# Three first-layer blocks before the first second-layer block, channels 128 to 191 convolved in two token halves, operands in named homes

## The chip, the core and the metric

The kernel runs on one core of a Trainium2 chip. The metric is the device time of one execution in microseconds. The kernel before takes 1253.04 us, the median of three runs (1252.96 to 1254.81).

## What is computed

A causal depthwise convolution (7 taps, softmax of a weight per head, 8 heads of 24 channels) over 2 x 4096 tokens of 192 channels, then two layers on the 8192 tokens, all in float32:

```
w = softmax(weight, axis=-1)                       # (8, 7)
x[t, c] = sum_k w[head(c), k] * x_pad[t + k, c]    # causal, zeros ahead of the first token
g = x @ w_gate ; val = x @ w_val                   # 192 -> 1536 each
y = (silu(g) * val) @ w_out                        # 1536 -> 192
h = y @ w_in                                       # 192 -> 2048
out = where(h > 0, h, exp(min(h, 0)) - 1) @ w_out2 # 2048 -> 192
```

## The kernel before

The 8192 tokens are cut into 16 blocks of 512 (TB). Each block goes through layer 1 (called A0 to A15 here: 12 steps, one for each 128 columns of d_ff) and layer 2 (B0 to B15: 8 steps of two such groups). Channels lie on partitions, tokens along the free axis.

Every float32 operand of a matmul is split in two fp32r parts, hi and lo (a cast on ACT, then a subtraction on DVE), and three products hi*hi, hi*lo, lo*hi are summed in PSUM. An operand x or y of a block is a pair of tiles with three slots of 512 columns: slot 0 holds channels 0 to 127, slot 1 the same channels with the two 64-partition halves swapped (two transfers from SBUF to SBUF, `turn`, L417), slot 2 channels 128 to 191 on both halves. A step of a layer issues nine pairs of matmuls into PSUM (`Into.nine`, L316), one matmul of a pair on the lower and one on the upper 64 rows of the array, then the activation and the split of h (`swiglu` and `elus`, `split`: L535, L539, L569 to L581, L509, L513), and two steps later the five pairs of the output product of each group (`OutOf.ten`, L358). A layer-1 block therefore has 12 x 18 + 12 x 10 matmuls, a layer-2 block 8 x 18 + 16 x 10.

The weights arrive as 34 pieces of int64 words (float64 in memory), which `piece` turns into fp32r hi and lo parts on the chip: transfers by the SP queue (L235), one scaling on ACT (L239), a shift, a sign and a low-bits step on DVE (L243, L247, L253), then hi on ACT (L258) and lo on DVE (L261). Pieces 0 to 17 belong to layer 1, 18 to 33 to layer 2. All of them have to be through once; this is work of the first 165 us only.

`load_x` brings a block of x into the tile xs (L438, L440; 128 channels in one transfer, channels 128 to 191 twice, to both halves), `conv` runs seven taps over it for g = 0 (channels 0 to 127) and g = 1 (channels 128 to 191, the same numbers on both halves of the partitions): the last tap on ACT (L466), six on DVE (L469), each 128x512.

The order of all instructions is written by a planner, `Plan`. Each piece of work is a task with an engine, a cost (`pitch`, the time that it holds its engine, and `ready`, the time until its result can be used) and its dependences; `Plan.run` hands out tasks engine by engine in the order of a simulated time, the one with the longest remaining chain first. PE's tasks keep the order in which they were written, which is that of the list `stages` (L685): A0, A1, B0, A2, B1, A3, B2 and so on up to A15, B14, B15. On the chip every engine then follows its own list in order and waits by semaphores. Buffers are rings: the tiles of all x and y share a ring of three (`x_p`), reused in the order in which they were made; PSUM has 4 banks for the first products, xs 2 tiles, the words 4.

Of the kernel before, what the change touches and what calls it, by code (L numbers as in the profile page):

```python
# [126 lines left out]
def tile_conv_swiglu_elu(ctx: ExitStack, tc: tile.TileContext, x, weight, words, out, FF1, FF2):  # L127
# [8 lines left out]
    G = D // H  # L136
    HALO = K - 1
    NU = {1: FF1 // P, 2: FF2 // P}
    assert D == P + HALF
# [80 lines left out]
    def piece(moves, halves, serves):  # L220

        k = len(pieces)
        pieces.append(k)
        st_b, f_b = plan.buffer("ws", 4), plan.buffer("wf", 4)
        box = {}

        def bring(i):
            if i == 0:  # L230
                box["st"] = ws_p.tile([P, C, 2], I32, tag="ws", name=f"words{k}")
            (r, g), (r_in, g_in) = moves[i]
            w = words[k].rearrange("p (g c w) -> p g c w", g=3, w=2)
# [29 lines left out]
        came = [  # L263
            move(lambda i=i: bring(i), new=[st_b] if i == 0 else (), uses=[] if i == 0 else [st_b], ready=3.6)
            for i in range(len(moves))
        ]
        for i in came[1:]:
            i.behind.append(came[0])
        t = act(scale, came, new=[f_b], uses=[st_b], pitch=0.45, ready=0.6)
        t = dve(shift, [t], uses=[f_b], pitch=0.29, ready=0.4)  # L270
        t = dve(sign, [t], uses=[f_b, st_b], pitch=0.49, ready=0.6)
        t = dve(low, [t], uses=[f_b, st_b], pitch=0.49, ready=0.6)
        his, los = [], []
        for pick, hi, lo in halves:
# [96 lines left out]
    class Operand:  # L371

        def __init__(self, name):
            self.name = name
            self.bufs = [plan.buffer(f"x{q}", 3) for q in ("hi", "lo")]
            self.tiles = [None, None]
            self.slots = {}

        def make(self, q):
            self.tiles[q] = x_p.tile([P, 3, TB], F32R, tag=f"x{'hi lo'.split()[q]}", name=f"{self.name}{q}")

        def write(self, s, value, needs, uses, n):

# [23 lines left out]
            if s == 0:  # L409
                for q, done in ((0, h), (1, l)):  # L410
# [2 lines left out]
                        for r, r_in in ((lower, upper), (upper, lower))  # L413
                    ]

    def turn(t, r, r_in, n):
        nc.sync.dma_start(out=raw(t[r, 1, :n]), in_=raw(t[r_in, 0, :n]))  # L417

    def load_x(b):
        i, t0, n = blocks[b]  # L420
        a = HALO if t0 == 0 else 0
        c = slice(t0 - HALO + a, t0 + n)
        buf = plan.buffer("xs", 2)
        box = {}

        def make():
            box["t"] = xs_p.tile([P, 2, HALO + TB], F32, tag="xs", name=f"xs{b}")

        def pad():
            make()  # L430
            nc.gpsimd.memset(box["t"][:, :, 0:a], 0.0)

        def bring(k):
            if k == 0 and not a:
                make()
# [6 lines left out]
        padded = [pool(pad, new=[buf], pitch=0.1, ready=0.2)] if a else []  # L442
        came = []
        for k in range(3):
            new = [buf] if k == 0 and not a else []
            came.append(move(lambda k=k: bring(k), new=new, uses=[] if new else [buf], ready=3.4))
            if k:
                came[k].behind.append(came[0])
            came[k].behind += padded
        xs[b] = box, buf, [padded + came[:1], padded + came[1:]]  # L450

    X = {}

    def conv(b, g):

        n = blocks[b][2]
        src, src_b, came = xs[b]
        acc_b = plan.buffer("cv", 2)
        box = {}

        def tap(k, eng=None):
            s = src["t"][:, g, k : k + n]
            w = taps[:, g, k : k + 1]
            if k == HALO:
                box["acc"] = cv_p.tile([P, TB], F32, tag="cv", name=f"cv{b}_{g}")
                nc.scalar.mul(box["acc"][:, :n], s, w)  # L466
                return
            acc = box["acc"][:, :n]
            nc.vector.scalar_tensor_tensor(out=acc, in0=s, scalar=w, in1=acc, op0=ALU.mult, op1=ALU.add)  # L469

        t = act(lambda: tap(HALO), came[g], new=[acc_b], uses=[src_b], pitch=0.62, ready=0.78)
        for k in range(HALO):
            t = dve(lambda k=k: tap(k), [t], uses=[src_b, acc_b], pitch=0.67, ready=0.8)
        if g == 0:
            X[b] = Operand(f"x{b}")
        X[b].write(2 * g, lambda: box["acc"][:, :n], [t], [acc_b], n)


    Y = {}
# [144 lines left out]
    def middle(b, *ends):  # L624
        n = blocks[b][2]
        (s1, b1, o1), (s2, b2, o2) = gathered((1, b), (f"y1_{b}", f"y2_{b}"), ((o_p, "o1"), (y_p, "y")), ends, n)
        Y[b] = Operand(f"y{b}")
# [54 lines left out]
        conv(0, g)  # L682
    load_table(AF.Silu)

    stages = [(1, 0)]  # L685
    for b in range(NB):
        if b + 1 < NB:
            stages.append((1, b + 1))
        stages.append((2, b))
    steps = [[]]  # L690
    for i, (layer, b) in enumerate(stages):
        if layer == 1 and b + 1 < NB:
            load_x(b + 1)
            for g in range(2):
                conv(b + 1, g)
# [8 lines left out]
        for u in us:  # L704
            products_out(u)

    plan.run({"pe": 5.0, "act": 5.0, "dve": 5.0, "pool": 3.0, "sp": 0.6}, PATIENCE)


# [43 lines left out]
```

## Time and profile before

| | |
|---|---|
| median of three runs | 1253.04 us |
| the profiled execution | 1253.94 us, of which span 1252.1 us |
| PE busy | 1216.1 us, 97% of the span |
| DVE busy | 1011.8 us, 81% |
| ACT busy | 822.7 us, 66% |

PE is the TensorE matmul engine, PEld its weight loads, DVE the vector engine, ACT the scalar engine, SP the queue that issues the transfers. Busy shares are means over a start-up and a steady part that have different limits, so the profile is read by stage below. "us" in a row is a length, the first number of a timeline row its start. In the views by stretch, x counts the instructions that touch the stretch, those at its edges too; PEclk is the granted TensorE clock as a share of 2.4 GHz.

### The profile page before, as it was taken

Reading aid. Unit: us, or ns where it says so; the run is one execution under the profiler, and the core shown is the slowest. Engines: PE = TensorE matmul, PEld = TensorE weight load, DVE = VectorE, ACT = ScalarE, POOL = GpSimd, SP = SyncE. Lnnn points to the kernel's source line nnn. Section 1 sums busy time; section 2 is a strip of 40 time slices with the busy share of each in tenths; the row PEclk is TensorE's granted clock in tenths of the full one; section 3 lists DMA queues with packets and bytes.
Section 4 is the critical chain, followed back from the end, with each engine's and each line's share of the span. In section 5 each row is a group of like instructions: output and inputs, shape, how many; then the busy total and the mean of one; then the engine's idle time right before and its main releaser. Section 6 shows DMA issues by size and latency. Waiting matters only on the chain.

```text
span 1252.1 us, 25084 instructions
## 1 busy us (share of the span) xinstructions
PE 1216.1 (97%) x10244; PEld 1127.8 (90%) x10244; DVE 1011.8 (81%) x1661; ACT 822.7 (66%) x1505; POOL 1.6 (0%) x11
## 2 busy tenths in 40 slices
PE   4989899999999999999999999999999999999998
PEld 3568689889999999999899999999999999999996
DVE  7999997979779596986959789695977959485697
ACT  4567757658476584857758486674857658485675
POOL 0000000000000000000000000000000000000000
PEclk9989999999999999999999999999999999999999
DMA  6433111111101010010101001010100101000000
GB/s 170 138 102 119 47 39 44 30 44 35 31 18 43 5 35 31 18 47 18 31 19 35 31 18 48 3 41 22 28 20 19 31 1 35 14 18 14 15 13 18
DMA packets 29795, 46.53 MB, mean 37 GB/s; under 512 B 4848, under 2 KB 12528, under 8 KB 29680
## 3 DMA queue, kind: packets, MB, share of 16 engines
q1 hardware_dynamic: 29664, 44.93, 13.7%
q8 instruction: 80, 1.31, 0.4%
q14 instruction: 35, 0.29, 0.1%
q10 hardware_dynamic: 16, 0.00, 0.0%
HBM read 21.84 MB, written 6.29 MB: 22 GB/s over the span
## 4 chain that ended last, share of the span: by engine, by line
PE 87%; DVE 9%; DMA 1%; issue 1%; ACT 1%; SPq 0%; DVEq 0%; ACTq 0%
PE c L358 38%; PE ph L316 19%; PE pv L316 16%; PE pg L316 14%; DVE cv L469 2%; DVE t L581 1%; DVE h L513 1%; DVE t L577 1%; DMA words<-in_words_dram 1%; DVE w L253 1%; DVE w L247 1%; DVE t L539 0%; DVE w L243 0%; DVE out L261 0%; SPq L235 0%
## 5 line engine op out<-in xcount | busy, mean ns | idle before, releaser
L358 PE MATMUL c<-h,out 64*128 64x512 f32 x4480 | 620.5, 393 | 8.8 <-DVE out L261 4.2
L358 PEld LDWEIGHTS c<-h,out 64*128 64x128 f32 x4480 | 515.8, 185 | 47.7 <-DVE h L513 9.4
L316 PE MATMUL pg<-x,in1hi 64*128 64x512 f32 x1152 | 394.7, 396 | 15.9 <-ACT in1hi L258 15.2
L316 PE MATMUL pv<-x,in1hi 64*128 64x512 f32 x1152 | 395.3, 397 | 0.1
L509 ACT CAST h<-t 128x512 fp32r<-128x512 f32 x448 | 280.0, 627 | 161.6 <-DVE t L539 138.6
L513 DVE TENSOR_TENSOR h<-t,h 128x512 fp32r<-128x512 f32 x448 | 307.5, 686 | 92.3 <-ACT h L509 90.8
L316 PE MATMUL ph<-y,in2hi 64*128 64x512 f32 x1536 | 307.4, 393 | 1.4 <-DVE t L581 1.1
L316 PEld LDWEIGHTS pg<-x,in1hi 64*128 64x128 f32 x1152 | 214.9, 187 | 28.0 <-ACT in1hi L258 16.7
L316 PEld LDWEIGHTS ph<-y,in2hi 64*128 64x128 f32 x1536 | 218.7, 184 | 12.9 <-DVE t L581 3.8
L316 PE MATMUL pg<-x,in1lo 64*128 64x512 f32 x576 | 228.8, 397 | 0.3
L316 PE MATMUL pv<-x,in1lo 64*128 64x512 f32 x576 | 228.4, 397 | 0.0
L316 PEld LDWEIGHTS pv<-x,in1hi 64*128 64x128 f32 x1152 | 215.4, 187 | 9.9 <-DVE t L539 0.8
L539 DVE TENSOR_TENSOR t<-t,pv 128x512 f32<-128x512 f32 x192 | 131.2, 683 | 112.8 <-ACT t L535 112.6
L535 ACT ACTIVATE t<-pg 128x512 f32<-128x512 f32 x192 | 114.7, 597 | 160.1 <-PE pg L316 137.4
L316 PE MATMUL ph<-y,in2lo 64*128 64x512 f32 x768 | 205.6, 392 | 0.0
L569 ACT ACTIVATE th<-ph 128x512 f32<-128x512 f32 x256 | 155.6, 608 | 50.0 <-PE ph L316 41.7
L577 DVE SCALAR_TENSOR_TENSOR t<-t,th 128x512 f32<-128x512 f32 x256 | 171.7, 685 | 15.2 <-ACT t L573 15.2
L581 DVE SCALAR_TENSOR_TENSOR t<-ph,t 128x512 f32<-128x512 f32 x256 | 170.0, 685 | 2.0
L573 ACT ACTIVATE t<-ph 128x512 f32<-128x512 f32 x256 | 155.3, 607 | 0.0
L469 DVE SCALAR_TENSOR_TENSOR cv<-xs,taps,cv 128x512 f32<-128x512 f32 x192 | 139.0, 743 | 3.9 <-ACT cv L466 2.8
L316 PEld LDWEIGHTS ph<-y,in2lo 64*128 64x128 f32 x768 | 120.5, 185 | 3.9 <-DVE in2lo L261 0.6
L316 PEld LDWEIGHTS pg<-x,in1lo 64*128 64x128 f32 x576 | 107.6, 187 | 7.9 <-DVE in1lo L261 3.3
(47 smaller groups left out, 501.1 us busy)
## 6 DMA issues: line engine op xcount, KB each, us to landing
x<-x SPq DMA_DIRECT2D x64, 128.0 KB, 2.3
y<-y SPq DMA_DIRECT2D x64, 128.0 KB, 2.3
words<-in_words_dram SPq DMA_DIRECT2D x14, 384.0 KB, 3.2
words<-in_words_dram SPq DMA_DIRECT2D x40, 128.0 KB, 2.8
out_dram<-o SPq DMA_DIRECT2D x16, 256.0 KB, 2.0
xs<-in_x_dram SPq DMA_DIRECT2D x14, 259.0 KB, 2.9
xs<-in_x_dram SPq DMA_DIRECT2D x28, 129.5 KB, 3.2
words<-in_words_dram SPq DMA_DIRECT2D x40, 64.0 KB, 2.5
```

Source lines behind the costliest of these rows:

```text
L247: nc.vector.scalar_tensor_tensor(out=i, in0=box["st"][:, :, 1], scalar=-(2**31), in1=i, op0=ALU.bitwise_and, op1=ALU.bitwise_or)
L316: nc.tensor.matmul(p[:, :n], w[r, k, s], m[r, s, :n], start=i == 0, stop=i == len(seq) - 1)
L358: nc.tensor.matmul(p[:, :n], lhs[r], m[r, :n], start=first, stop=last)
L469: nc.vector.scalar_tensor_tensor(out=acc, in0=s, scalar=w, in1=acc, op0=ALU.mult, op1=ALU.add)
L509: nc.scalar.copy(parts[u][0][:, :n], live[u][0]["t"][:, :n])
L513: nc.vector.tensor_tensor(out=parts[u][1][:, :n], in0=live[u][0]["t"][:, :n], in1=raw(parts[u][0][:, :n]), op=ALU.subtract)
L535: nc.scalar.activation(out=box["t"][:, :n], in_=box["p"][0][:, :n], func=AF.Silu)
L539: nc.vector.tensor_tensor(out=t, in0=t, in1=box["p"][1][:, :n], op=ALU.mult)
L569: nc.scalar.activation(out=own["th"][:, :n], in_=box["p"][a][:, :n], func=AF.Tanh, scale=0.5)
L573: nc.scalar.activation(out=own["t"][:, :n], in_=box["p"][a][:, :n], func=AF.Exp)
L577: nc.vector.scalar_tensor_tensor(out=t, in0=t, scalar=1.0, in1=th, op0=ALU.add, op1=ALU.mult)
L581: nc.vector.scalar_tensor_tensor(out=t, in0=box["p"][a][:, :n], scalar=0.0, in1=t, op0=ALU.max, op1=ALU.min)
```

## The change

Three things change, and with them the planner's order of nearly all instructions.

The list `stages` gets a lead of three: A0, A1, A2, B0, B1, A3, B2, A4, B3 and on as before. Against the list before, A2 and B0 change places; from A3 on the two are the same.

Channels 128 to 191 are convolved in halves of the tokens: xs holds the first 256 tokens of a block on partitions 0 to 63 and the second 256 on partitions 64 to 127, so that the six taps of g = 1 are 128x256 and the tap on ACT too. `spread` then writes hi and lo of the two halves in place (two casts on ACT and two subtractions on DVE, each 64x256), and four transfers from SBUF to SBUF copy each half to the other 64 partitions. Before, the same slot took one cast and one subtraction of 128x512 and no transfer.

Operand tiles are no longer a ring: `settle` gives every x and y one of three homes by the stage in which the earlier occupant is last used. The planner also charges a transfer with 0.62 instead of 0.4 us of SP's time.

```
+LEAD = 3
-    x_p = ctx.enter_context(tc.tile_pool(name="xp", bufs=3))
+    x_p = ctx.enter_context(tc.tile_pool(name="xp", bufs=1))
-    def move(emit, needs=(), new=(), uses=(), pitch=0.4, ready=2.8):
+    def move(emit, needs=(), new=(), uses=(), pitch=0.62, ready=2.9):
...
+            self.bufs = [plan.buffer(f"x{q}{home}", 1) for q in ("hi", "lo")]
...
+        def spread(self, value, done, buf, n):
+            half = n // 2
+            places = (lower, slice(0, half)), (upper, slice(half, n))
+            first = self.slots[0, 0][0], self.slots[1, 0][0]
+            his, los = [], []
+            for r, c in places:
+                def hi(r=r, c=c):
+                    nc.scalar.copy(self.tiles[0][r, 2, c], value()[r, :half])
+                def lo(r=r, c=c):
+                    nc.vector.tensor_tensor(
+                        out=self.tiles[1][r, 2, c], in0=value()[r, :half], in1=raw(self.tiles[0][r, 2, c]), op=ALU.subtract
+                    )
+                h = act(hi, [done], uses=[self.bufs[0], buf], pitch=0.33, ready=0.45)
+                l = dve(lo, [done, h], uses=[*self.bufs, buf], pitch=0.34, ready=0.47)
...
+            for q, own in enumerate((his, los)):
+                other = []
+                for (r, c), (r_in, _), t in zip(places, places[::-1], own):
+                    def send(q=q, r=r, c=c, r_in=r_in):
+                        nc.sync.dma_start(out=raw(self.tiles[q][r_in, 2, c]), in_=raw(self.tiles[q][r, 2, c]))
+                    other.append(move(send, [t], uses=[self.bufs[q]]))
+                self.slots[q, 2] = [*own, *other]
...
         def bring(k):
-            if k == 0 and not a:
-                make()
-            t = box["t"]
             if k == 0:
-                nc.sync.dma_start(out=t[:, 0, a : HALO + n], in_=x[i, 0:P, c])
-            else:
-                nc.sync.dma_start(out=t[(lower, upper)[k - 1], 1, a : HALO + n], in_=x[i, P:D, c])
+                box["t"] = xs_p.tile([P, 2 * HALO + TB + TB // 2], F32, tag="xs", name=f"xs{b}")
+            skip = a if k < 2 else 0
+            first, m = (0, n) if k == 0 else ((k - 1) * half, half)
+            rows = slice(0, P) if k == 0 else slice(P, D)
+            src = x[i, rows, t0 + first - HALO + skip : t0 + first + m]
+            nc.sync.dma_start(out=at(k, skip, HALO + m), in_=src)
...
+        m, c0 = ((n, 0), (n // 2, HALO + TB))[g]
...
+    stages = [(1, b) for b in range(min(LEAD, NB))] + [(2, b) for b in range(LEAD - 1)]
+    for b in range(LEAD - 1, NB):
+        if b + 1 < NB:
+            stages.append((1, b + 1))
+        stages.append((2, b))
+    home, last = {}, {}
+    for i, (layer, b) in enumerate(stages):
+        last["xy"[layer - 1], b] = i
+    holds = [None] * 3
+    def settle(what, i):
+        free = [h for h in range(3) if holds[h] is None or last[holds[h]] < i]
+        home[what] = h = max(free, key=lambda h: last[holds[h]] if holds[h] else -1)
+        holds[h] = what
...
-    stages = [(1, 0)]
-    for b in range(NB):
-        if b + 1 < NB:
-            stages.append((1, b + 1))
-        stages.append((2, b))
```

What the planner makes of it is seen at three places. Names are tiles: wordsN and wN are weight piece N as words and on the way to fp32r, xsN the input of block N, cvN_g its convolution, x0N the hi and x1N the lo tile of block N, h1_L_b_j the lo part of group j of block b in layer L, t the activation, in1, in2, out1, out2 the finished weights.

The first transfers of the SP queue, before: words of the first pieces (seven transfers in all), then the input.

```order
L235 DMA words1_135<-in_words_dram 64x2x256
L235 DMA words1_135<-in_words_dram 64x256
L235 DMA words1_135<-in_words_dram 64x2x256
L438 DMA xs0_139<-in_x_dram 128x512
L440 DMA xs0_139<-in_x_dram 64x512 x2
```

And now, from the first transfer on:

```order
L474 DMA xs0_130<-in_x_dram 128x512
L474 DMA xs0_130<-in_x_dram 64x256
L474 DMA xs0_130<-in_x_dram 64x262
L236 DMA words0_134<-in_words_dram 64x2x256
L236 DMA words0_134<-in_words_dram 64x256
```

The input now goes first, the first words behind it.

DVE at the end of the first convolution, before (the shift and the sign of piece 0 stand ahead of the convolution there):

```order
L469 SCALAR_TENSOR_TENSOR cv0_1_162<-xs0_139,taps_106,cv0_1_162 128x512 x2
L396 TENSOR_TENSOR x01_186<-cv0_0_155,x00_181 128x512
L253 SCALAR_TENSOR_TENSOR w0_152<-words0_130,w0_152 128x384
L469 SCALAR_TENSOR_TENSOR cv0_1_162<-xs0_139,taps_106,cv0_1_162 128x512
L243 TENSOR_SCALAR w1_166<-w1_166 128x384
L261 TENSOR_TENSOR in1lo_109<-w0_152,in1hi_108 128x384
```

And now:

```order
L506 SCALAR_TENSOR_TENSOR cv0_1_145<-xs0_130,taps_106,cv0_1_145 128x256 x3
L398 TENSOR_TENSOR x01_182<-cv0_0_141,x00_177 128x512
L244 TENSOR_SCALAR w0_157<-w0_157 128x384
L248 SCALAR_TENSOR_TENSOR w0_157<-words0_134,w0_157 128x384
L431 TENSOR_TENSOR x01_182<-cv0_1_145,x00_177 64x256 x2
L254 SCALAR_TENSOR_TENSOR w0_157<-words0_134,w0_157 128x384
L244 TENSOR_SCALAR w1_168<-w1_168 128x384
```

The taps of g = 1 are half as wide, the shift and the sign of piece 0 stand behind the convolution, and the lo part of slot 2 is two pieces of 64x256.

DVE in the middle of B0, before: weight pieces 25, 27, 28 and 30 between the steps of the layer.

```order
L581 SCALAR_TENSOR_TENSOR t2_0_7_1676<-ph0_7_1604,t2_0_7_1676 128x512
L261 TENSOR_TENSOR in2lo_111<-w28_1498,in2hi_110 128x384
L247 SCALAR_TENSOR_TENSOR w27_1455<-words27_1372,w27_1455 128x384
L261 TENSOR_TENSOR out2_113<-w25_1367,out2_113 128x2x128
L261 TENSOR_TENSOR out2_113<-w25_1367,out2_113 128x2x64
L253 SCALAR_TENSOR_TENSOR w27_1455<-words27_1372,w27_1455 128x384
L513 TENSOR_TENSOR h1_2_0_6_1758<-t2_0_6_1652,h0_2_0_6_1719 128x512
L577 SCALAR_TENSOR_TENSOR t2_0_8_1712<-t2_0_8_1712,th0_8_1705 128x512
L243 TENSOR_SCALAR w30_1760<-w30_1760 128x384
L247 SCALAR_TENSOR_TENSOR w30_1760<-words30_1459,w30_1760 128x384
```

And now, at the same group 7 of B0:

```order
L647 SCALAR_TENSOR_TENSOR t2_0_7_2254<-ph0_7_2183,t2_0_7_2254 128x512
L706 TENSOR_TENSOR y2_2197<-y2_2197,y2_2_2112 128x512
L579 TENSOR_TENSOR h1_2_0_6_2308<-t2_0_6_2227,h0_2_0_6_2297 128x512
L643 SCALAR_TENSOR_TENSOR t2_0_8_2291<-t2_0_8_2291,th0_8_2284 128x512
```

The weight pieces are gone from B0: the last of them now stands ahead of its first step, inside A2.

## Rows read from the trace of the kernel before

**Rows 1.** The page, part 1: busy us, share of the span, instructions.

```profile
PE 1216.1 (97%) x10244; PEld 1127.8 (90%) x10244; DVE 1011.8 (81%) x1661; ACT 822.7 (66%) x1505; POOL 1.6 (0%) x11
```

**Rows 2.** The page, part 4: the chain that ended last, by engine.

```profile
PE 87%; DVE 9%; DMA 1%; issue 1%; ACT 1%; SPq 0%; DVEq 0%; ACTq 0%
```

**Rows 3.** By stretch: A0, A1, B0, A2, B1; then A4's neighbours, steady.

```profile
19.30:74.00 54.70, 48.59 (x316) 33.08 (x317) 51.13 (x105) 30.91 (x65) 0.00 (x0) 0.94 0.51 144
74.00:114.40 40.40, 39.91 (x338) 32.20 (x337) 37.96 (x75) 25.77 (x51) 0.00 (x0) 1.00 0.41 112
114.40:157.50 43.10, 37.95 (x288) 27.95 (x285) 42.74 (x81) 36.10 (x74) 0.00 (x0) 1.00 0.21 62
157.50:201.30 43.80, 43.70 (x356) 40.65 (x358) 36.16 (x62) 22.39 (x41) 0.00 (x0) 0.96 0.15 42
201.30:235.20 33.90, 33.78 (x288) 28.08 (x286) 32.11 (x53) 29.63 (x57) 0.00 (x0) 1.00 0.14 30
...
276.50:309.60 33.10, 33.10 (x287) 31.00 (x285) 30.11 (x50) 28.76 (x55) 0.00 (x0) 1.00 0.09 20
309.60:351.00 41.40, 41.40 (x359) 41.33 (x357) 29.23 (x46) 20.75 (x36) 0.11 (x1) 1.00 0.13 34
```

**Rows 4.** Timeline of DVE: five places, start, length, instruction.

```profile
24.43 0.69 DVE L539 TENSOR_TENSOR t<-t,pv 128x512 f32<-128x512 f32 x1
...
77.72 0.68 DVE L539 TENSOR_TENSOR t<-t,pv 128x512 f32<-128x512 f32 x1
...
119.76 0.35 DVE L243 TENSOR_SCALAR w<-w 128x384 int32<-128x384 int32 x1
120.03 0.68 DVE L577 SCALAR_TENSOR_TENSOR t<-t,th 128x512 f32<-128x512 f32 x1
...
167.26 0.68 DVE L539 TENSOR_TENSOR t<-t,pv 128x512 f32<-128x512 f32 x1
```

**Rows 5.** Timeline of DVE, 104 to 108 us: a stretch without a gap.

```profile
104.35 0.55 DVE L261 TENSOR_TENSOR in2lo<-w,in2hi 128x384 fp32r<-128x384 f32 x1
104.82 0.42 DVE L261 TENSOR_TENSOR out<-w,out 128x256 fp32r<-128x256 f32 x1
105.15 0.68 DVE L513 TENSOR_TENSOR h<-t,h 128x512 fp32r<-128x512 f32 x1
105.75 0.28 DVE L261 TENSOR_TENSOR out<-w,out 128x128 fp32r<-128x128 f32 x1
105.95 0.55 DVE L253 SCALAR_TENSOR_TENSOR w<-words,w 128x384 int32<-128x384 int32 x1
106.42 0.74 DVE L469 SCALAR_TENSOR_TENSOR cv<-xs,taps,cv 128x512 f32<-128x512 f32 x1
107.09 0.68 DVE L539 TENSOR_TENSOR t<-t,pv 128x512 f32<-128x512 f32 x1
```

**Rows 6.** Timeline of SP's queue, the first transfers.

```profile
0.80 4.69 SPq L235 DMA_DIRECT2D words<-in_words_dram  x7
5.54 0.59 SPq L438 DMA_DIRECT2D xs<-in_x_dram  x1
```

**Rows 7.** Timeline of DVE at the start; in brackets the wait and its releaser.

```profile
4.90 0.17 DVE L213 COPY taps<-ptaps 128x14 f32<-128x14 f32 x1 [1.17 <-PE ptaps L212]
9.71 7.75 DVE L469 SCALAR_TENSOR_TENSOR cv<-xs,taps,cv 128x512 f32<-128x512 f32 x11 [2.75 <-ACT cv L466]
```

**Rows 8.** Timeline of PE: its first product.

```profile
19.27 0.79 PE L316 MATMUL pg<-x,in1hi 64*128 64x512 f32 x1 [14.41 <-ACT in1hi L258]
```

**Rows 9.** The page, part 6: a transfer between partitions, KB, us to landing.

```profile
x<-x SPq DMA_DIRECT2D x64, 128.0 KB, 2.3
```

**Rows 10.** By stretch, columns as in rows 3: around the lowest clock.

```profile
60.00:66.00 6.00, 3.13 (x22) 1.79 (x20) 6.00 (x13) 2.28 (x6) 0.00 (x0) 1.00 0.35 111
66.00:72.00 6.00, 5.69 (x24) 3.94 (x24) 5.96 (x11) 2.38 (x4) 0.00 (x0) 0.54 0.22 66
```

**Rows 11.** ACT's casts of x (L390): what they waited for, us, times.

```profile
  PE ph L316: 6.4, 11
```

More of the change, by code (lines that the diff above doesn't have):

```diff
@@ L138, in tile_conv_swiglu_elu @@
     NU = {1: FF1 // P, 2: FF2 // P}
-    assert D == P + HALF
+    assert D == P + HALF and TB % 2 == 0
     C = 2 * D
@@ L263, in piece @@
         came = [
-            move(lambda i=i: bring(i), new=[st_b] if i == 0 else (), uses=[] if i == 0 else [st_b], ready=3.6)
+            move(lambda i=i: bring(i), new=[st_b] if i == 0 else (), uses=[] if i == 0 else [st_b], ready=3.3)
             for i in range(len(moves))
@@ L371, in tile_conv_swiglu_elu, with __init__ @@
     class Operand:
-        def __init__(self, name):
+        def __init__(self, name, home):
             self.name = name
-            self.bufs = [plan.buffer(f"x{q}", 3) for q in ("hi", "lo")]
+            self.home = home
+            self.bufs = [plan.buffer(f"x{q}{home}", 1) for q in ("hi", "lo")]
             self.tiles = [None, None]
@@ L381, in make @@
         def make(self, q):
-            self.tiles[q] = x_p.tile([P, 3, TB], F32R, tag=f"x{'hi lo'.split()[q]}", name=f"{self.name}{q}")
+            self.tiles[q] = x_p.tile([P, 3, TB], F32R, tag=f"x{q}{self.home}", name=f"{self.name}{q}")
         def write(self, s, value, needs, uses, n):
@@ L414, in write @@
                     ]
+        def spread(self, value, done, buf, n):
[12 more added lines that the diff above has]
+                l = dve(lo, [done, h], uses=[*self.bufs, buf], pitch=0.34, ready=0.47)
+                h.behind.append(first[0])
+                l.behind.append(first[1])
+                his.append(h)
+                los.append(l)
+            for q, own in enumerate((his, los)):
[5 more added lines that the diff above has]
+                self.slots[q, 2] = [*own, *other]
     def turn(t, r, r_in, n):
@@ L420, in load_x, with at @@
         i, t0, n = blocks[b]
+        half = n // 2
         a = HALO if t0 == 0 else 0
-        c = slice(t0 - HALO + a, t0 + n)
         buf = plan.buffer("xs", 2)
         box = {}
-        def make():
-            box["t"] = xs_p.tile([P, 2, HALO + TB], F32, tag="xs", name=f"xs{b}")
-        def pad():
-            make()
-            nc.gpsimd.memset(box["t"][:, :, 0:a], 0.0)
+        def at(k, c0, c1):
+            t = box["t"]
+            return t[:, c0:c1] if k == 0 else t[(lower, upper)[k - 1], HALO + TB + c0 : HALO + TB + c1]
         def bring(k):
-            if k == 0 and not a:
-                make()
-            t = box["t"]
             if k == 0:
-                nc.sync.dma_start(out=t[:, 0, a : HALO + n], in_=x[i, 0:P, c])
-            else:
-                nc.sync.dma_start(out=t[(lower, upper)[k - 1], 1, a : HALO + n], in_=x[i, P:D, c])
[L442 to L450, printed above, removed]
+                box["t"] = xs_p.tile([P, 2 * HALO + TB + TB // 2], F32, tag="xs", name=f"xs{b}")
[4 more added lines that the diff above has]
+            nc.sync.dma_start(out=at(k, skip, HALO + m), in_=src)
+        came = [
+            move(lambda k=k: bring(k), new=[] if k else [buf], uses=[buf] if k else [], ready=3.2) for k in range(3)
+        ]
+        pads = []
+        if a:
+            for k in range(2):
+                pads.append(pool(lambda k=k: nc.gpsimd.memset(at(k, 0, a), 0.0), uses=[buf], pitch=0.1, ready=0.2))
+                pads[k].behind.append(came[0])
+        for k in (1, 2):
+            came[k].behind.append(came[0])
+        xs[b] = box, buf, [pads[:1] + came[:1], pads[1:] + came[1:]]
     X = {}
@@ L459, in conv, with tap @@
         box = {}
-        def tap(k, eng=None):
-            s = src["t"][:, g, k : k + n]
+        def tap(k):
+            s = src["t"][:, c0 + k : c0 + k + m]
             w = taps[:, g, k : k + 1]
@@ L465, in tap @@
                 box["acc"] = cv_p.tile([P, TB], F32, tag="cv", name=f"cv{b}_{g}")
-                nc.scalar.mul(box["acc"][:, :n], s, w)
+                nc.scalar.mul(box["acc"][:, :m], s, w)
                 return
-            acc = box["acc"][:, :n]
+            acc = box["acc"][:, :m]
             nc.vector.scalar_tensor_tensor(out=acc, in0=s, scalar=w, in1=acc, op0=ALU.mult, op1=ALU.add)
-        t = act(lambda: tap(HALO), came[g], new=[acc_b], uses=[src_b], pitch=0.62, ready=0.78)
+        less = 0.0 if g == 0 else 0.27
+        t = act(lambda: tap(HALO), came[g], new=[acc_b], uses=[src_b], pitch=0.62 - less, ready=0.78 - less)
         for k in range(HALO):
-            t = dve(lambda k=k: tap(k), [t], uses=[src_b, acc_b], pitch=0.67, ready=0.8)
+            t = dve(lambda k=k: tap(k), [t], uses=[src_b, acc_b], pitch=0.67 - less, ready=0.8 - less)
         if g == 0:
-            X[b] = Operand(f"x{b}")
-        X[b].write(2 * g, lambda: box["acc"][:, :n], [t], [acc_b], n)
+            X[b] = Operand(f"x{b}", home["x", b])
+            X[b].write(0, lambda: box["acc"][:, :n], [t], [acc_b], n)
+        else:
+            X[b].spread(lambda: box["acc"], t, acc_b, n)
+    stages = [(1, b) for b in range(min(LEAD, NB))] + [(2, b) for b in range(LEAD - 1)]
[11 more added lines that the diff above has]
+        holds[h] = what
+    settle(("x", 0), 0)
+    for i, (layer, b) in enumerate(stages):
+        if i and stages[i - 1][0] == 1:
+            settle(("y", stages[i - 1][1]), i)
+        if i + 1 < len(stages) and stages[i + 1][0] == 1:
+            settle(("x", stages[i + 1][1]), i)
     Y = {}
@@ L626, in middle @@
         (s1, b1, o1), (s2, b2, o2) = gathered((1, b), (f"y1_{b}", f"y2_{b}"), ((o_p, "o1"), (y_p, "y")), ends, n)
-        Y[b] = Operand(f"y{b}")
+        Y[b] = Operand(f"y{b}", home["y", b])
         Y[b].write(0, lambda: o1["o"][:, :n], [s1], [b1], n)
@@ L683, in tile_conv_swiglu_elu @@
     load_table(AF.Silu)
-    stages = [(1, 0)]
-    for b in range(NB):
-        if b + 1 < NB:
-            stages.append((1, b + 1))
-        stages.append((2, b))
     steps = [[]]
     for i, (layer, b) in enumerate(stages):
-        if layer == 1 and b + 1 < NB:
-            load_x(b + 1)
+        if i + 1 < len(stages) and stages[i + 1][0] == 1:
+            load_x(stages[i + 1][1])
             for g in range(2):
-                conv(b + 1, g)
+                conv(stages[i + 1][1], g)
         if i and stages[i - 1][0] != layer:
@@ L705, in tile_conv_swiglu_elu @@
             products_out(u)
-    plan.run({"pe": 5.0, "act": 5.0, "dve": 5.0, "pool": 3.0, "sp": 0.6}, PATIENCE)
+    plan.run({"pe": 5.0, "act": 5.0, "dve": 5.0, "pool": 3.0, "sp": 0.8}, PATIENCE)
 def kernel(x, weight, moe_w_gate, moe_w_val, moe_w_out, moe2_w_in, moe2_w_out):
```

## The prediction

> **What bounds the kernel now.** I read the page's busy shares first, then the chain, then the stretches stage by stage, and last the timeline of DVE. PE is busy 97% of the span [rows 1] and carries 87% of the chain, DVE 9% [rows 2]. The reader should not stop there, since shares mix a start and a steady part. The stretches show the parting [rows 3]; their columns are length, then busy PE, PEld, DVE, ACT, POOL, then clock. In the steady part PE has no gap: a B stage of 284 matmuls (by the program's order) takes 33.1 us, an A stage of 356 takes 41.4 us, both 0.1164 us a matmul, with DVE at 30.1 and 29.2 us. Nothing that only spares DVE can gain there. In the first stages it is the other way round. A0 (316 matmuls, 36.8 us at that pace) takes 54.7 us with DVE busy 51.1 of them; B0 (284, 33.1 us) takes 43.1 us with DVE busy 42.7. A2 (356) takes 43.8 instead of 41.4 us at a clock of 0.96. So the losses are the start to 19.3 us, 17.9 us in A0, 1.3 in A1, 10.0 in B0, 2.4 in A2 and 0.8 in B1, and the cause in A0 and B0 is DVE, which turns the weights into fp32r beside the layers' own work.
>
> **DVE's work, priced from start to start.** In a stretch without a gap [rows 5] an operation of 512 columns holds DVE 0.60 us, a tap 0.67, a 384-column weight step 0.47, an out piece of 256 columns 0.33 and of 128 columns 0.20; the shift 0.27 (119.76 to 120.03) [rows 4]. I count the instructions that stand in DVE's order from the first layer operation of one stage to that of the next. Before, A0 to A1: 25 full, 12 taps, 38 weight steps, 14 shifts, 6 and 6 out pieces, 47.9 us; the trace needs 77.72 - 24.43 = 53.3 us for it [rows 4], 1.11 times as much, with waits for ACT in between. A1: 39.1 us. B0: 51 full, 4 taps, 17 weight steps, 6 shifts, 5 and 5 out pieces, 45.6 us; the trace needs 167.26 - 120.03 = 47.2 us [rows 4], 1.036 times, with PE waiting. So counted work times 1.04 is what a saturated DVE takes.
>
> **The change, part by part.**
>
> 1. The exchange of A2 and B0. PE's matmuls from A1 to the start of A3 are 1260 in both orders (before 336 + 284 + 356 + 284, now 336 + 336 + 284 + 304): 146.7 us at the steady pace, against 235.2 - 74.0 = 161.2 us now. That is 14.5 us to be had, if DVE follows. Its work by the new order: A1 37.9 us (30 full, 3 taps, 6 half taps, 23 weight steps, 9 shifts, the rest small) against 39.1 us of PE; A2 36.4 against 39.1; B0 32.5 (53 full, 2 of 64x256) against 33.1; B1 35.3 (52 full, 5 taps, 2 half taps) against 35.4. The 12.3 us of weight work that B0 held (17 x 0.47 + 6 x 0.27 + 5 x 0.53) now lies in A1 and A2, where the layer leaves DVE 11 to 14 us free. The sums with the factor 1.036 are 39.3, 37.7, 33.7 and 36.6 us: over PE's by 0.2, under it, 0.6 and 1.2. Work that is over in one stage is mostly not wanted at once, but DVE goes in order; I charge the 2.0 us in full. What is late next is therefore DVE in B1, by little. The gain is 14.5 - 2.0 = 12.5 us.
>
> 2. The half-width taps. No 128x256 tap stands in the trace. Below, it is the 0.33 us of a plain operation of 256 columns, above, the 0.47 us of a 384-column step [rows 5]; I take 0.40, as the tap exceeds a plain operation by 0.07 at 512 columns. Six taps save 6 x 0.27 = 1.6 us a block, and the two 64x256 subtractions cost 2 x 0.34 against 0.60. In the sums above that is included; from A3 on it buys nothing, PE having no gap there to give back. The bounds move the first 12 half taps by +-0.8 us and the later 14 by +-1.0 us. The Trainium skill (Perfetto Trace Analysis, Optimizing Scalar/DVE Operations) gives DVE about 60 ns on SBUF for each instruction beside its columns; by that my estimate for a half tap is 0.33 us, and the sum would come out 1.8 us lower. For the full tap the same estimate is 0.59 us, where the trace shows 0.67, so I do not go by it.
>
> 3. The start. SP now brings the input ahead of the first words; before, seven transfers went first and the input was issued at 5.54 us [rows 6]. The convolution began at 9.71 us, waiting for ACT's tap and that for the input; the taps' coefficients were there at 5.07 [rows 7]. From the issue to the first tap on DVE went 4.2 us, so that an input issued at 0.8 us would let DVE start at 5.0; now the coefficients come last, and with ACT's tap behind them (0.8 us, estimated from a tap's 0.74 on DVE) it starts near 5.9 us, 3.8 earlier. Its taps take 6 x 0.67 + 6 x 0.40 = 6.4 us, some 6.9 with the dependent ones, then the lo part 0.60, shift and sign 1.0 (they lay in the idle time before), two half subtractions 0.7, the low bits 0.5: 15.6 us, and the cast of the first weight 0.5 more. The first product comes at 16.1 to 16.4 us instead of 19.27 [rows 8], 2.9 to 3.2 earlier. Against this stand eight transfers of X0 between partitions instead of four, 0.62 us each on SP and 2.3 us to landing [rows 9]: the last, of slot 1 lo, lands near 20.2 us, when the first nine pairs want it at 19.5, so that some 0.5 us of the lead is lost again. I take 2.6 us, bounds 1.4 (both transfers of a full landing late) and 3.8 (the whole lead of the convolution). Words later by three transfers (1.9 us) are hidden behind the convolution.
>
> 4. A0. DVE's work there is 47.5 against 47.9 us: 0.4 us. The new SP prices in the planner may also take away part of the 3.6 us in which DVE idled there (54.7 - 51.1); I take none, bound 3.6. X1's slot 2 now needs four transfers after its subtractions, queued ahead of slot 1 lo: 2 x 0.62 us later on SP, hidden as the half taps make X1 ready sooner by as much. If that cover is gone it costs 1.2 us once.
>
> 5. The homes. From A3 on they give the same tile lifetimes as the ring. X3 must wait until B0's last first product, two stages ahead of its use. Nothing. The 12 further spreads (8 transfers instead of 4 a block) lie some 70 us ahead of their use: nothing either.
>
> **The sum.** A1 starts 2.6 + 0.4 = 3.0 us earlier; A3 starts 3.0 + 12.5 = 15.5 us earlier; behind it PE's order is the same. The profiled execution took 1253.94 us and would take 1238.4; it lies 0.9 above the median of the runs, so I say 1237.5 us.
>
> **The rivals.**
>
> DVE gives back half. The two B stages now stand side by side, and DVE's work is within 2 us of PE's time in each. If DVE reaches there only what it reached in A0 (factor 1.11), A1 to A3 takes 142.1 x 1.11 = 157.7 us, the gain is 161.2 - 157.7 + 3.0 = 6.5 us, 1246.5 us. For it: one operation more or less in line decides, and DVE's list is fixed. Against it: in B0 before, as full, the factor was 1.036; the excess in A0 came with weights still arriving, and in the B stages none arrive now.
>
> The clock. After the thin stretch of 60 to 66 us (PE busy 3.13 of 6) the granted clock fell to 0.54, that is to the lower level for nearly all of 66 to 72 us; 24 matmuls stand where the steady pace has 52 [rows 10], 28 x 0.1164 = 3.2 us. Less idle time in A0 might leave the clock up; with the 3.6 us in which DVE idled that is 6.8 us more: 1231 us. For it: DVE's work before A1 is less and comes earlier. Against it: A0 remains DVE's. The Trainium skill (TensorE: Matmul & The Clock Gate, What's actually happening) says that activity releases the throttle, so that a thinner start would cost clock too and a denser one give it back; rows 10 agree as to the fall.
>
> No gain: the wait only moves, and B0 and B1 end DVE-bound by as much as the exchange gave. That takes a factor of (161.2 + 3.0)/142.1 = 1.16, above anything in the trace: 1253 us.
>
> Slower: the hand-over of homes. ACT's cast of each x stands between the activations of the last B steps and waits for PE's last reading of the home; now 11 of them wait 0.6 us each on average, off PE's path [rows 11]. If the fixed home makes each of 13 wait 1.5 us longer, with the activations queued behind it and PE behind those, that is 19 us, 4 more than the gain: 1257 us. It decides from 1.2 us a block. Against it: in the new order the cast stands at the same place between the same activations.
>
> **How the numbers follow.** Forecast (1232 to 1243): 0.72. DVE gives half back: 0.12. Clock and idle time: 0.07. No gain: 0.05. Slower: 0.04. A range of 1232 to 1245 leaves out about 0.2. A measurement of this kernel tells 0.2% (2.5 us) from no change, so faster is 0.91, same 0.05, slower 0.04.
>
> **What would show it.** First product near 16.2 us; A1 starting near 71.0 us; A1, A2, B0, B1 at 39, 39, 34 and 36 us with DVE nearly full throughout; A3 near 219.7 us instead of 235.2; then the same pace to the end. I am wrong if B0 or B1 takes over 38 us, if the clock drops in them, or if PE waits for x in the steady part.

## The result, and the profile after

The changed kernel takes 1242.63 us (median of 4 runs, 1242.40 to 1243.06) against 1253.38 us before on the same chip (4 runs, 1252.96 to 1254.81): a ratio of 0.991, 95% interval 0.9897 to 0.9923. That is 10.75 us, where 15.5 were forecast. The profiled execution took 1243.06 us with a span of 1241.3.

The page's busy shares, after, answer to [rows 1]:

```profile
PE 1214.1 (98%) x10244; PEld 1070.5 (86%) x10244; DVE 992.5 (80%) x1677; ACT 821.1 (66%) x1517; POOL 1.6 (0%) x13
```

They say next to nothing: the same 10244 matmuls, PE a little fuller. The stretches by stage say where the time went. Columns as in [rows 3]; A0, A1, A2, B0, B1, and then B2 and A4:

```profile
16.50:68.40 51.90, 47.50 (x318) 33.17 (x319) 50.50 (x108) 31.28 (x67) 0.00 (x0) 0.93 0.55 162
68.40:108.30 39.90, 39.48 (x335) 31.88 (x333) 39.31 (x78) 26.17 (x55) 0.00 (x0) 1.00 0.45 123
108.30:148.10 39.80, 39.69 (x344) 32.10 (x341) 39.34 (x81) 26.09 (x54) 0.00 (x0) 1.00 0.27 74
148.10:181.50 33.40, 33.40 (x290) 31.33 (x288) 31.51 (x54) 29.16 (x56) 0.00 (x0) 1.00 0.14 34
181.50:216.70 35.20, 35.20 (x304) 30.34 (x302) 34.93 (x59) 28.44 (x57) 0.00 (x0) 1.00 0.12 30
258.80:291.90 33.10, 33.10 (x287) 31.24 (x285) 30.11 (x50) 28.73 (x55) 0.00 (x0) 1.00 0.09 20
291.90:334.20 42.30, 42.20 (x358) 36.33 (x356) 28.12 (x47) 20.81 (x37) 0.13 (x2) 1.00 0.14 36
```

The reader should see three things. A0 is 51.9 us instead of 54.7 and starts earlier. A1, A2, B0 and B1 come to 148.3 us instead of 161.2 [rows 3]. But the steady A stage, the last row, is 42.3 us where it was 41.4 [rows 3], and that with DVE *less* busy (28.1 instead of 29.2 us): something that the change was said not to touch got slower. By stage starts: A3 begins at 216.73 us instead of 235.16, which is 18.4 us gained, and B14, the last B stage but one, at 1161.44 instead of 1172.18, 10.7 us gained. Between them 7.7 us go lost, in the eleven A stages from A3 to A13; A14 and A15, which have no taps of a later block beside them, take 41.4 us as before.

Where in the stage? The waits of PE's weight loads from 230 to 1040 us (us in total, times, longest), first before:

```profile
PEld c L358 <- DVE h L513: 1.6, 7, 0.3
```

then after:

```profile
PEld c L359 <- DVE o L683: 4.1, 10, 0.4
PEld c L359 <- DVE p L683: 3.4, 10, 0.3
PEld c L359 <- ACT o L679: 1.5, 8, 0.2
```

o and p are the tiles into which ACT and DVE gather what the B block before has left in its four PSUM buffers c: ACT copies one buffer of each pair out (L613, in the changed kernel L679), DVE adds the other (L617, now L683). There are four such buffers, and the A stage behind can begin its own sums in each of them only when that one has been read. Its first ten output products (c<-h) want them at the end of its third step. The timeline up to there, A4 before, which starts at 309.64 us (start, length, engine and instruction; the rows of the input products and others left out):

```profile
314.36 0.69 DVE L396 TENSOR_TENSOR x<-cv,x 128x512 fp32r<-128x512 f32 x1
...
315.56 2.32 DVE L469 SCALAR_TENSOR_TENSOR cv<-xs,taps,cv 128x512 f32<-128x512 f32 x3
...
317.80 0.68 DVE L539 TENSOR_TENSOR t<-t,pv 128x512 f32<-128x512 f32 x1
...
319.73 0.68 DVE L617 TENSOR_TENSOR p<-p,c 128x512 f32<-128x512 f32 x1
...
320.32 0.68 DVE L617 TENSOR_TENSOR o<-o,c 128x512 f32<-128x512 f32 x1
...
320.56 1.46 PE L358 MATMUL c<-h,out 64*128 64x512 f32 x10
320.92 0.69 DVE L513 TENSOR_TENSOR h<-t,h 128x512 fp32r<-128x512 f32 x1
```

and after, the same steps of A4, which starts at 291.94 us (in brackets the wait and what ended it):

```profile
296.69 0.41 DVE L431 TENSOR_TENSOR x<-cv,x 64x256 fp32r<-64x256 f32 x1
...
297.26 0.69 DVE L579 TENSOR_TENSOR h<-t,h 128x512 fp32r<-128x512 f32 x1 [0.16 <-ACT h L575]
...
297.96 0.42 DVE L431 TENSOR_TENSOR x<-cv,x 64x256 fp32r<-64x256 f32 x1
...
298.42 2.33 DVE L506 SCALAR_TENSOR_TENSOR cv<-xs,taps,cv 128x512 f32<-128x512 f32 x3
...
302.32 0.68 DVE L579 TENSOR_TENSOR h<-t,h 128x512 fp32r<-128x512 f32 x1
...
302.87 2.33 PE L359 MATMUL c<-h,out 64*128 64x512 f32 x10
302.92 0.68 DVE L683 TENSOR_TENSOR p<-p,c 128x512 f32<-128x512 f32 x1
303.02 0.29 PEld L359 LDWEIGHTS c<-h,out 64*128 64x128 f32 x3 [0.19 <-ACT o L679]
303.52 0.68 DVE L683 TENSOR_TENSOR o<-o,c 128x512 f32<-128x512 f32 x1
...
303.65 0.18 PEld L359 LDWEIGHTS c<-h,out 64*128 64x128 f32 x1 [0.34 <-DVE p L683]
304.11 0.47 DVE L506 SCALAR_TENSOR_TENSOR cv<-xs,taps,cv 128x256 f32<-128x256 f32 x1
...
304.25 0.52 PEld L359 LDWEIGHTS c<-h,out 64*128 64x128 f32 x5 [0.41 <-DVE o L683]
304.51 0.68 DVE L728 TENSOR_TENSOR o<-o,p 64x512 f32<-64x512 f32 x1
```

Before, DVE did the two adds and then the low part of the hidden unit (L513); now that low part (L579) comes first and the adds behind it. The ten output products then take 2.33 instead of 1.46 us, with three waits of 0.94 us together. A second cause stands earlier in the same rows. The lo part of slot 2 is two subtractions now, with a wait for ACT beside them, and the taps behind it start 6.48 us into the stage instead of 5.92, so everything behind on DVE is 0.56 us later. With the 0.60 us of the low part ahead, and 0.27 us less for a tap of half the width, that makes the 0.89 us by which the first add, p, comes later in its stage (10.98 instead of 10.09 us). Why the planner chose this order, no run shows. Note that PE counts as busy all the while (42.20 of 42.30 us): the loss stands in the length of a group and in the loads' waits, not in PE's busy share.

### The profile page after: what moved, and what is told of

It reads as the page before. It is cut to its first block, busy times and chain, and to the rows that moved or that the text cites. A ratio compares the mean times of both kernels' runs of the same rounds, so it can differ in the third digit from the quotient of the medians.

```text
span 1241.3 us, 25261 instructions
## 1 busy us (share of the span) xinstructions
PE 1214.1 (98%) x10244; PEld 1070.5 (86%) x10244; DVE 992.5 (80%) x1677; ACT 821.1 (66%) x1517; POOL 1.6 (0%) x13
## 5 line engine op out<-in xcount | busy, mean ns | idle before, releaser
L359 PE MATMUL c<-h,out 64*128 64x512 f32 x4480 | 640.2, 394 | 4.8 <-DVE out L262 1.4
L579 DVE TENSOR_TENSOR h<-t,h 128x512 fp32r<-128x512 f32 x448 | 307.1, 686 | 98.2 <-ACT h L575 96.6
L317 PEld LDWEIGHTS ph<-y,in2hi 64*128 64x128 f32 x1536 | 225.3, 185 | 13.1
L317 PE MATMUL ph<-y,in2lo 64*128 64x512 f32 x768 | 212.0, 391 | 0.0
L317 PEld LDWEIGHTS ph<-y,in2lo 64*128 64x128 f32 x768 | 126.5, 185 | 6.2
L317 PEld LDWEIGHTS pv<-x,in1lo 64*128 64x128 f32 x576 | 107.3, 186 | 15.6
L506 DVE SCALAR_TENSOR_TENSOR cv<-xs,taps,cv 128x512 f32<-128x512 f32 (+1 forms) x192 | 113.8, 610 | 2.9 <-ACT cv L503 0.9
```

Source lines behind the costliest of these rows:

```text
L317: nc.tensor.matmul(p[:, :n], w[r, k, s], m[r, s, :n], start=i == 0, stop=i == len(seq) - 1)
L359: nc.tensor.matmul(p[:, :n], lhs[r], m[r, :n], start=first, stop=last)
L579: nc.vector.tensor_tensor(out=parts[u][1][:, :n], in0=live[u][0]["t"][:, :n], in1=raw(parts[u][0][:, :n]), op=ALU.subtract)
```

## The experiments

The theory after these rows, P: the change gains 18.4 us up to A3, and gives 7.7 back by the *place* of the gather on DVE, which the halved tokens have moved. The rivals: T (traffic), the four added transfers between partitions in each block slow PE, whatever the order; H, something else does it, which means the lead or the homes in e1 to e3, and the halved tokens' own instructions in e5 and e7. The table has the starts of A0 and A3, the time from A3 to B14 (all from PE's timeline), and the time of the runs. "SP price" stands for all that the planner assumes of transfers: SP's time and the times until they can be used. The runs of before beside the experiments had medians of 1254.23 us (e1 to e4) and 1254.63 us (e5 to e8), 7 runs each.

| kernel | tokens | lead | SP price | A0 | A3 | A3 to B14 | us (4 runs) | ratio to before, 95% |
|---|---|---|---|---|---|---|---|---|
| before | whole | 2 | old | 19.27 | 235.16 | 937.0 | 1253.38 | |
| after | halved | 3 | new | 16.56 | 216.73 | 944.7 | 1242.63 | 0.9897 to 0.9923 |
| e1 | halved, gather first | 3 | new | 16.56 | 216.90 | 938.7 | 1236.35 | 0.9841 to 0.987 |
| e2 | halved | 2 | new | 16.92 | 223.60 | 944.3 | 1249.27 | 0.9945 to 0.9975 |
| e3 | whole | 3 | new | 17.71 | 218.78 | 936.3 | 1236.62 | 0.9841 to 0.9874 |
| e4 | halved | 3 | old | 17.94 | 222.84 | 944.7 | 1248.80 | 0.9936 to 0.9966 |
| e5 | whole, gather late | 3 | new | 17.64 | 219.22 | 941.9 | 1242.37 | 0.9889 to 0.9918 |
| e6 | whole | 3 | old | 19.38 | 223.08 | 936.3 | 1241.52 | 0.9884 to 0.9914 |
| e7 | halved in blocks 0 to 2 | 3 | new | 16.57 | 216.92 | 936.7 | 1235.17 | 0.9831 to 0.9861 |
| e8 | whole | 2 | new | 17.33 | 227.94 | 936.5 | 1246.58 | 0.9921 to 0.9954 |

**e1, the gather first.** An order is written into the planner: the hidden unit's two parts of that step go behind the copies and the adds.

```diff
             done.append((s, buf, box))
+            u = list(split_of)[-1]
+            if key[0] == 2 and u[0] == 1:
+                h, l = split_of[u][1]
+                h.behind.append(c)
+                l.behind.append(s)
```

> The changed kernel with one more rule for the planner: in the second step of an A stage the hi cast and the lo part of that step's group stand behind ACT's copies and DVE's sums that empty the four PSUM banks of the B block before. Nothing is left out. Theory P (the place): each A stage from A3 to A12 takes 42.1 to 42.3 us instead of 41.4 because PE's first output product waits for these banks, which the hi cast on ACT and the lo part on DVE now delay; freed first, these stages take 41.4 us and the time is 1242.6 - 10 x 0.8 = 1234.6 us (1234 to 1236). Rival T (traffic): the four added transfers between partitions in each block slow PE; then the order does not matter and it stays 1242.6 us. Rival H (homes and lead): it stays at 1242.6 us too.

Measured 1236.35 us (1235.48 to 1237.16), 6.3 us less than the changed kernel, with A3 at nearly the same time (216.90). P holds for most of the loss; T and H, which expected no change, do not. The median lies 0.35 us above P's range. What is left to P's 1234.6 shows in the loads' waits of this kernel, same columns and stretch:

```profile
PEld c L359 <- DVE o L683: 3.1, 10, 0.4
PEld c L359 <- DVE h L579: 0.7, 3, 0.3
```

The wait for p is gone, that for the second add, o, is still there, and A3 to B14 is 1.7 us longer than before, 2.4 longer than with whole tokens (e3). This rest goes with the two subtractions: with the order put back, p's add still starts 10.37 us into A4 (302.50 us), 0.28 later than before, which is the 0.56 less the 0.27 above. That reading is from rows alone; no run took the subtractions away by themselves.

**e2, halved tokens without the lead**, and **e4, the changed kernel with the planner's old prices of a transfer**:

```diff
-LEAD = 3
+LEAD = 2
```
```diff
-    def move(emit, needs=(), new=(), uses=(), pitch=0.62, ready=2.9):
+    def move(emit, needs=(), new=(), uses=(), pitch=0.4, ready=2.8):
...
-    plan.run({... "sp": 0.8}, PATIENCE)
+    plan.run({... "sp": 0.6}, PATIENCE)
```

> The changed kernel with a lead of two, so that the stages stand as before (A0, A1, B0, A2, ...); token halves, homes and transfer prices stay. All theories: A1 starts some 5.6 us earlier than before; B0 is still DVE-bound, 42.6 us of counted work instead of 45.6, 3 us less. P and T: the A stages of the steady part still take 42.2 us, 8 us lost, so 1253.4 - 8.6 + 8 = 1252.8 us (1251 to 1255). H (the lead or its homes cause the steady loss): 41.4 us a stage and 1244.8 us.

> The changed kernel with the planner's old prices of transfers (0.4 us of SP, 2.8 us to use, words 3.6, input 3.4). The input still goes first, three transfers ahead of the words. If the new prices gave part of the earlier A1 (5.6 us earlier, of which the forecast had 3.0), A0 gets longer by 1 to 2.6 us and the time is 1243.6 to 1245; if they did nothing, 1242.6. The steady A stages stay at 42.2 us by all theories.

Measured 1249.27 us for e2 and 1248.80 us for e4. Both figures were missed. In e2 the loss came as P and T had it: 7.3 us from A3 on, with A3 to A13 at 42.1 to 42.3 us each. So the lead does not cause it. Missed was the gain ahead of it: A3 came 11.6 us earlier without any lead, where 8.6 were expected. e4 is 6.2 us slower than the changed kernel, all of it ahead of A3 (222.84 instead of 216.73): the price is no trifle. The start of e4 shows why, here ACT and DVE:

```profile
13.33 0.54 ACT L240 ACTIVATE w<-words 128x384 f32<-128x384 f32 x1 [0.82 <-DMA words<-in_words_dram]
13.78 0.60 ACT L392 CAST x<-cv 128x512 fp32r<-128x512 f32 x1
...
14.41 0.69 DVE L398 TENSOR_TENSOR x<-cv,x 128x512 fp32r<-128x512 f32 x1 [1.28 <-ACT x L392]
```

and the changed kernel at the same place:

```profile
11.73 0.62 ACT L392 CAST x<-cv 128x512 fp32r<-128x512 f32 x1
...
13.05 0.68 DVE L398 TENSOR_TENSOR x<-cv,x 128x512 fp32r<-128x512 f32 x1
```

SP issues the words at 8.49/13 = 0.65 us each in both (13 transfers in 8.49 us, the row is below). With 0.4 in its table the planner has the words come sooner than they do and puts one more conversion (L240) ahead of x's cast; ACT goes in order, waits for that word until 13.33, and DVE and the first product (17.94 instead of 16.56) wait with it. From 15 to 75 us the waits of PE for operands (the first product's own left out) are 9.1 us in e4 and 4.2 in the changed kernel. e4 also has one more fall of the clock: behind a stretch with PE busy 3.75 of 6 us (30 to 36) the granted clock is 0.75 from 36 to 42 us, where the changed kernel has 1.00. I estimate from these rows that some 1.7 us of the 6.2 went that way.

**e3, the lead with whole tokens.** load_x and conv are those of the kernel before; homes, lead and prices stay.

> The changed kernel with channels 128 to 191 convolved over whole tokens as before (128x512 taps, no added transfers); lead, homes and prices stay. P and T: the steady A stages take 41.4 us. The input is fifth in SP's queue instead of first, a start about 2 us earlier than before. DVE's counted work in A1, A2, B0, B1 is 38.6, 38.7, 33.2 and 35.1 us, times 1.036 it exceeds PE's 39.1, 39.1, 33.1 and 35.4 by 0.9, 1.0, 1.3 and 1.0: 150.9 us instead of 161.2. So 1253.4 - 2 - 10.3 = 1241 us (1239 to 1243). H: 8 us more, 1249 us.

Measured 1236.62 us (1235.91 to 1237.23): 6 us less than the changed kernel, and below both expectations (1241 and 1249). A3 is 2.05 us later, and nothing is lost behind it, with the lead and the homes in place, so H in its first form (1249 us) falls. The halved tokens, which the change put beside the lead, cost it 6 us net.

**e5, whole tokens with the gather late.** The same few lines as in e1, turned round, in the kernel of e3:

```diff
             done.append((s, buf, box))
+            u = list(split_of)[-1]
+            if key[0] == 2 and u[0] == 1:
+                h, l = split_of[u][1]
+                c.behind.append(h)
+                s.behind.append(l)
```

> Whole tokens with the lead (1236.62 us), and the two copies and two adds that empty the four PSUM buffers of a B block are put behind the high and the low part of the hidden unit of the second step of the next A block, where the planner had them ahead. Theory P (the place of these adds on VectorE sets the 0.8 us that the ten A stages from A3 to A12 lose in the changed kernel): those ten stages grow from 41.4 to about 42.2 us and the time to 1244 us (1242 to 1246), with TensorE's weight loads waiting for the adds o and p as in the changed kernel. Rival H (the loss comes with the halved tokens' own instructions, four casts, subtracts and sends where there were two and more, wherever the adds stand): nothing changes, 1236.6 us (1235.5 to 1238).

Measured 1242.37 us (1241.94 to 1242.71), 5.75 us slower than e3, with not one instruction of the halved tokens in it. The same waits as in the changed kernel appear (loads of PE, 230 to 1040 us):

```profile
PEld c L359 <- DVE p L678: 4.6, 11, 0.4
PEld c L359 <- DVE o L678: 1.3, 7, 0.2
```

So the order alone makes most of the loss, and H, which expected no change, falls as it was stated. From A3 to B14 the order costs 5.6 us here (941.9 instead of 936.3), where the halved tokens cost 8.4 (944.7 instead of 936.3) and leave 2.4 with the order put back (e1). That rest is what is true of H. A stage loses 0.5 us here (41.9 us) rather than the 0.8 that I expected, since DVE and ACT are not 0.56 us late besides: o's add comes 0.62 us later in A4 than p's did before, which is the low part ahead and no more, and ACT's copies, for which loads waited 1.5 us in the changed kernel, now come in time. (It is eleven stages, A3 to A13; the expectation says ten.)

**e6, the lead alone, at the old price**, and **e8, the new price alone, without the lead.** e6 is e3 with the edit of e4; e8 is e3 with the edit of e2. Both keep the homes, which no run takes out.

> Whole tokens with the lead, and the planner's old prices for a transfer (an issue on SP 0.4 us instead of 0.62, and the start after it). This leaves of the change the exchange of stages and the homes alone. Theory S (the new price orders SP's issues of the words and x in A0 better, and that is a term of its own beside the exchange): A0 loses the 4 us that it had gained, and the exchange alone is left: 1253.7 - 12.5 = 1241 us (1240 to 1243). Rival L (the start's gain came from the lead, which gives the planner more to put into A0): 1236.6 us (1235.5 to 1238).

> The planner's new prices and the homes alone: whole tokens, and the stages in the order A0 A1 B0 A2 B1 as in the kernel before. Theory S: A0 ends some 4.2 us earlier, as with the lead, and this goes through to the end: 1253.7 - 4.2 = 1249.5 us (1247 to 1251). Rival W (B0 waits for VectorE's work, and what A0 gains is lost there): 1253.7 us (1252.5 to 1255). Rival L (the start's gain needs the lead): A0 as before, 1253.7 us as well, but with the first product of A1 at 74 us.

Measured 1241.52 us for e6: theory S and the forecast's own term, 12.1 us at A3 (235.16 to 223.08) where the prediction had 12.5 for the exchange. Measured 1246.58 us for e8, beyond S: 7.2 us at A3, of which A0 gave 4.6 (ACT's first activation of A1 at 72.29 instead of 76.89 us) and B0 2.0 more (109.89 to 150.91, 41.0 us instead of 43.0), as A1, which starts earlier, takes weight work out of B0: of the operations of 384 columns, the shifts aside, B0 holds 8 instead of 17 and A1 30 instead of 21, while A0 holds 45 in both. L falls, W too. The two overlap: 12.1 and 7.2 alone, 16.4 together (e3). That fits, since behind the exchange no weight work is left in B0 and its 2.0 us can't be gained twice.

**e7, halved tokens in the first three blocks only.** Both forms of load_x and conv stand in the kernel, and the block's number chooses:

```diff
+    HALVED = 3
+    def load_x(b):
+        (load_half if b < HALVED else load_whole)(b)
+    def conv(b, g):
+        (conv_half if b < HALVED else conv_whole)(b, g)
```

> The changed kernel with halved tokens in the first three blocks alone, and whole ones from the fourth on. Theory P: the start keeps what the halves give there (A3 began 2.05 us earlier in the changed kernel than in the one with whole tokens), and the ten stages that the halves had made longer are 41.4 us again: 1236.6 - 1.6 to 2.05 = 1234.8 us (1234 to 1236). Rival H (the halves cost or give by their instructions, block by block): three blocks of sixteen have them, so that the start gains little and the rest stays as with whole tokens, 1236.6 us (1236 to 1238).

Measured 1235.17 us (1234.80 to 1235.35), as P expected, and the lowest median of all (its interval overlaps those of e1 and e3): 19.5 us below the kernel before beside it (ratio 0.9846, 0.9831 to 0.9861). A4 in it (columns as in [rows 3]):

```profile
292.10:333.50 41.40, 41.40 (x360) 41.31 (x358) 29.11 (x45) 20.75 (x35) 0.14 (x2) 1.00 0.11 31
```

It has the start of the changed kernel (A3 at 216.92) and the steady pace of the kernel before [rows 3].

## Why the prediction was right, and where it was wrong

The direction and the range held, with 5 us of error in the forecast of 1237.5. That the range held is in part luck: its upper end was 0.4 us away, and two errors stand against each other. The start and A0 gave 2.6 us more than was forecast, without which the time would have been about 1245 us, and the steady part lost 7.7 us that the prediction put at nothing.

**The exchange of A2 and B0 (part 1): right in its size, not in its places.** 12.5 us were forecast; the lead alone gives 12.1 at A3 (e6), and in the changed kernel A1 to A3 shrank from 161.2 to 148.3 us, 12.9. The stages were forecast at 39, 39, 34 and 36 us and are 39.9, 39.8, 33.4 and 35.2; DVE is the nearly full engine in A1, A2 and B1 as said, and the 2.0 us charged for it were nearly what it took (148.3 - 146.7 = 1.6). They lay elsewhere, though: the sum had 0.6 and 1.2 of them in B0 and B1, and they came in A1 and A2, 0.8 and 0.7 over PE's 39.1, while B1 has no gap on PE at all. That this came out even is luck.

**The start (part 3): right.** The first taps were forecast at 5.9 us and came at 5.95, the first product at 16.1 to 16.4 and came at 16.56. Here the timeline of SP's queue, of DVE and of PE, which answer to [rows 6 to 8]:

```profile
0.80 1.65 SPq L474 DMA_DIRECT2D xs<-in_x_dram  x3
2.50 8.49 SPq L236 DMA_DIRECT2D words<-in_words_dram  x13
...
5.95 7.19 DVE L506 SCALAR_TENSOR_TENSOR cv<-xs,taps,cv 128x512 f32<-128x512 f32 x12 [0.86 <-ACT cv L503]
...
16.56 0.79 PE L317 MATMUL pg<-x,in1hi 64*128 64x512 f32 x1 [11.69 <-ACT in1hi L259]
```

**A0 (part 4): mis-sized.** I gave it 0.4 us, and to the new SP prices none of the 3.6 us in which DVE idled, with 3.6 as the bound. The price alone (with the homes), whole tokens and no lead, brings A1's first activation 4.6 us forward, 1.9 of that in the first product (17.33 instead of 19.27) and the rest in A0 (e8). In the changed kernel A1 starts at 68.39 us, 5.6 earlier than before, where start and A0 had 3.0 in the sum. The price is what the trace had shown all along: seven transfers in 4.69 us are 0.67 each [rows 6], against 0.4 in the old table.

**The half-width taps (part 2): the price right, the conclusion wrong.** A half tap holds DVE from 304.11 to 304.51, 0.40 us, as taken. The estimate from the Trainium skill (Perfetto Trace Analysis, Optimizing Scalar/DVE Operations) was 0.33 us; the measurement decides. But the step that failed is the sentence "from A3 on it buys nothing, PE having no gap there to give back", and in the sum "behind it PE's order is the same". PE's order was the same; DVE's was not. I priced the taps as DVE's time and found DVE with 12 us to spare in a steady A stage, and did not ask which instructions on DVE PE waits for there, and whether one of them would stand behind another now. The adds of the gather did, and came later besides, and that cost 7.7 us: 944.7 instead of 937.0 from A3 to B14. e5 shows the order by itself (5.6 us), e1 what is left without it (1.7 us against the kernel before, 2.4 against e3), e7 that the loss goes with the halved tokens of the later blocks. The order of DVE's instructions shows it, in the steady part; I had compared the first stages only. The same holds for the term of part 5 that put the 12 further spreads at nothing: their transfers do lie far ahead of their use, but their subtractions make DVE 0.56 us late in a steady A stage.

So 15.5 = 3.0 + 12.5 became 18.4 - 7.7 = 10.7 us.

**The homes (part 5): nothing speaks against it.** ACT's casts of x wait for PE's last reading as they did, against [rows 11]:

```profile
ACT x L392 <- PE ph L317: 5.9, 12, 0.5
```

The slower rival needed 1.2 us a block more there and is out. With the homes in them, e3, e6 and e8 keep the steady pace (936.3 to 936.5 us against 937.0).

**The other rivals.** DVE giving half back in B0 and B1 did not come (33.4 and 35.2 us). The clock in A0 was not spared either, so that rival is out as well; the same two stretches as in [rows 10], after:

```profile
60.00:66.00 6.00, 5.17 (x20) 3.27 (x22) 5.94 (x13) 4.08 (x9) 0.00 (x0) 0.53 0.47 119
66.00:72.00 6.00, 6.00 (x49) 4.74 (x47) 5.48 (x12) 3.35 (x9) 0.00 (x0) 0.90 0.73 210
```

The granted clock is 0.53 now in the first, so near the lower of its two levels (1.2 GHz), and 0.90 in the second, where it was 1.00 and 0.54: the same fall, about 6 us earlier, with A0 ending 5.6 us earlier. It came again behind a thin stretch, with PE busy 3.67 us of the 6 from 54 to 60 us. A second fall is gone, though, which the rival did not look at: A2 stood at 0.96 before, behind a B0 with PE busy 37.95 of 43.10 us [rows 3], and stands at 1.00 now, behind an A1 with PE busy 39.48 of 39.90 us. I estimate from these rows, 0.04 x 43.8, that 1.8 us of the exchange's gain are this clock given back.

## What to carry to other kernels

An engine with time to spare can still be late at one instruction: for each instruction on it that the bounding engine waits for (here the reads that set a PSUM buffer free), compare what stands ahead of it before and after, in the steady part too, since a loss there is paid once a block. When a planner's table is changed, compare its prices with the trace's; the new ones for SP's transfers (0.62 for 0.4 us an issue, where the trace has 0.65) were worth 8 us without the lead (e8) and 5 with it (e3 against e6). And a change of several parts is best run part by part: the best kernel here takes the halved tokens only where they help, in the first three blocks.

## What was not expected of the hardware

In the slowed A stage PEld is busy 36.33 us, with 356 loads, where before it was 41.33 with 357 [rows 3], and over the span 1070.5 instead of 1127.8 us [rows 1]; with e7 it is back at 41.31. That is 5 us a stage in records of loads for a loss of 0.9 us, so the loads' busy time is no measure of what they cost. The records are no shorter: a load takes 184 ns in this stage, against 185 before. They overlap: before, the loads of a pair start in turn (332.89 and 333.02 us), while behind the wait, up to the end of the stage, they start together (314.85 and 314.86), and busy time counts an overlap once. Why they stay together stays open; no run here was made for it.
